# Loading the first 256 tokens of queries and keys as f32 through SyncE and ScalarE, with a new global order, in a fused attention and gated-MLP kernel

## The chip, the cores and the metric

The kernel runs on one core of a Trainium2 chip. That core has a matrix engine (TensorE, PE), a vector engine (VectorE, DVE), a scalar engine (ScalarE, ACT), a general engine (GpSimd, POOL) and a synchronisation engine (SyncE, SP). Each engine runs its own instruction stream in order, and streams wait for each other only through semaphores. Transfers between HBM and on-chip memory are issued from the POOL, SP or ACT stream; those from POOL can change the data type on the way. The metric is the device time of one execution in microseconds (us), lower is better.

## The reference

The inputs are q, k, v of shape 4 x 8 x 768 x 64 (batch, heads, tokens, head size) and four weight matrices, all f32. Attention is computed first; heads 0, 2 and 6 see all earlier tokens, the other five see the 4 first tokens and a window of 64. Its result, 3072 tokens by 512 features, goes through a gated MLP.

```
scores = matmul(q, k.T) / 8
keep   = causal                                   # heads 0, 2, 6
keep   = causal & (key < 4 | query - key < 64)    # the other heads
x      = softmax(where(keep, scores, -1e9)) @ v   # as (3072, 512)

g    = x @ w_gate                                 # 512 x 1536
val  = x @ w_val                                  # 512 x 1536
gate = sigmoid(x @ w_res)                         # 512 x 512
out  = x + gate * ((gelu(g) * val) @ w_out)       # 1536 x 512
```

## The kernel before

**Chunks.** The 3072 tokens are worked on in six chunks of 512 (`CHUNKS`, lines 25 to 32), four tiles of 128 tokens each. Chunk 0 is tokens 0 to 511 of batch 0. For each chunk the kernel transposes q and k so that the head size lies on partitions (qT, kT), computes scores, exponentials, masks, the weighted sum of v, the normalisation, the transposed result xT, and then the gated MLP with f16 operands. Heads are taken in four pairs, `PAIRS = ((0, 2), (4, 6), (1, 3), (5, 7))`; chunk 0 takes them in the order pair 0, 2, 1, 3. Chunk 0 also works in two halves of 256 tokens: for its first four blocks of hidden features (f0 to f3), the gate and value products of half 0 are tasks of their own that can run while the attention of half 1 is not finished.

**Tasks and the order.** The program is a graph of tasks. Each task is a few instructions on one engine, with a list of tasks that it depends on. The order is not found when the kernel is built: the string table `PLAN` lists task numbers in one global order (lines 51 to 119), `PLACES` names the slot of each buffer, `schedule` (line 255) walks the list and appends each task to its engine's stream, and `assign_waits` puts in the semaphore waits that the dependencies need. A letter behind a number picks the engine where a task may run on more than one (a ACT, d DVE, g POOL, s SP). An entry w39 puts in 39 fillers (line 1414): matmuls of 256 columns on a zeroed tile that nobody reads and that keep PE busy. So an engine takes its tasks in the order of `PLAN`, and a task at the head of a stream that is not ready holds back all behind it.

**Loads of chunk 0.** All loads of q, k, v and of the weights are issued by POOL (`dma`, line 537; they appear as L539), because they turn f32 into f16 on the way. `loads_rows` (line 641) loads q and k of chunks 0 and 1. In chunk 0 the first 256 tokens (y = 0) come as two transfers of four heads for k and two for q, the next 256 tokens (y = 1) as one transfer each. Eight PE tasks `qkT` (L682, eight transposes of 128 by 64 each) and eight copies `qkE` (L693, 128 x 512, PSUM to SBUF, on DVE or ACT) then make kT and qT. `values` (line 606) loads v by tiles; the copies `vs` (L617) and `vk` (L598) arrange parts of v for the window heads. Nine small POOL instructions build the identity and two mask tiles (L497 to L525); the causal mask needs two of them, the window mask six and a copy on DVE (L508, `spread`).

**Attention and MLP lines.** Scores are L850, sink scores L941, exponentials L866 and L870, masks L902 (`mask0` for pair 0 is the first; it needs the causal mask). Weighted sums are L974 and L477, reciprocals L1028, `norm16` L1039, `norm` L1041, transposes of the result L1063 with their copies L1071 (`xE`). In chunks 3 to 5 half of that transpose is one DMA transpose issued by SP (L1054, `xD`). PE's gate and value products are L477 and L478: the helper `mm` issues one matmul over the whole array, or two over halves of 64 columns, as the mode of the array stands. DMA transposes of q and k from chunk 2 on are L726 (`dT`), also on SP.

**What PLAN gives around the start.** The streams before begin like this (names as above; K and Q for k and q, a and b for the two transfers of a matrix; gN and vN are the gate and value products of feature block fN, h0 and h1 the two halves):

```
POOL  K(y1) Ka Qa Kb Q(y1) 3 consts Qb v0 v1 3 consts wv0 4 consts v3 3 vk v2 vk wg0
      Q(chunk 1) Q(chunk 1) wg1 wv1 wg2 wv2 wr K K wo ...
PE    w39 T(y1 K) w2 T(y0 K) w4 T(y0 Q) T(y1 K) w6 scores ... w and T and scores mixed ...
      attention of h0 ... v1 v3 g3 g1 (h0), rest of h1, g0, T(chunk 1), g2 ...
DVE   E(y1 K) E(y0 Q) E(y1 K) E(y0 K) E(y1 Q) E(y1 Q) mask0 spread vs mask1 mask1 vs ...
```

77 fillers are placed, 39 of them at the very start.

Of the kernel before, what the change touches and what calls it, by code (L numbers as in the profile page):

```python
# [4 lines left out]
NHEAD = 8  # L5
# [425 lines left out]
def build_kernel(nc, q, k, v, w_gate, w_val, w_out, w_res, out):  # L431
# [153 lines left out]
    def values(b, a, z, base, each, on_engines=False):  # L585
# [43 lines left out]
        for lo in cuts:  # L629
            hi = lo + 1 if each else z  # L630
            ts = []
            for dst, src, off in ((0, 64, 1), (64, 0, 0)):
# [4 lines left out]
                ts[-1].late = 2.5  # L637
            for i in range(lo, hi):
                BB.vstok[i] = ts

    def loads_rows(c, si, b, a, z):

        BB = batch(b)
# [867 lines left out]
```

## Time and profile before

| | us |
|---|---|
| median of 3 runs | 266.2 (265.41 to 267.15) |
| profiled execution, its span from first to last instruction | 264.3 |
| PE busy | 254.5 |
| DVE busy | 210.8 |
| ACT busy | 155.3 |
| POOL busy | 106.8 |

The profile gives the execution's own time as its span. The median of the runs is 1.9 us above it. PE is busy in 96% of the span, but busy time also holds the fillers, and the share is a mean over stages with different limits; the start, up to about 30 us, has its own.

### The profile page before, as it was taken

What the parts mean: (1) busy time and instruction counts of PE and PEld (TensorE: products, weight loads), DVE (VectorE), ACT (ScalarE), POOL (GpSimd) and SP (SyncE); (2) the same over time, 40 slices, a digit from 0 to 9 for tenths busy, and PEclk for the clock granted to TensorE, in tenths of its full rate; (3) what the DMA queues carried; (4) which work ended last, traced back from release to release, by engine and by line L of the source; (5) the groups of instructions that cost most, each with busy time, mean ns of one, the idle gap of its engine ahead of it and who ended that gap; (6) DMA issues with size and microseconds to landing.
All of it is one profiled execution on the core that took longest, in us unless ns stands there. A gap on an engine that the chain in (4) does not pass through costs nothing.

```text
span 264.3 us, 8077 instructions
## 1 busy us (share of the span) xinstructions
PE 254.5 (96%) x3421; PEld 180.7 (68%) x3421; DVE 210.8 (80%) x473; ACT 155.3 (59%) x274; POOL 106.8 (40%) x145
## 2 busy tenths in 40 slices
PE   8999999999999999999998899999999998999993
PEld 5657655558567578667677477579588677778891
DVE  1499555999988978678999677999687976877985
ACT  1277534964554998564883356884655995445511
POOL 8996741990000998013976620711500111110021
PEclk9999999999999999999999999999999999999998
DMA  7999999999297999968999994899589509050004
GB/s 69 166 139 178 207 196 191 188 158 115 82 271 99 141 123 135 182 154 182 136 97 124 152 138 93 200 123 104 69 92 237 101 2 122 7 77 2 2 2 159
DMA packets 102067, 33.17 MB, mean 125 GB/s; under 512 B 88720, under 2 KB 97168, under 8 KB 102032
## 3 DMA queue, kind: packets, MB, share of 16 engines
q0 software_dynamic: 74704, 18.88, 77.3%
q1 hardware_dynamic: 26896, 13.26, 25.0%
q8 instruction: 27, 0.44, 0.7%
q10 hardware_dynamic: 432, 0.52, 0.5%
q14 instruction: 8, 0.07, 0.1%
HBM read 29.36 MB, written 10.49 MB: 151 GB/s over the span
## 4 chain that ended last, share of the span: by engine, by line
PE 87%; DVE 8%; DMA 3%; issue 1%; ACT 0%; DVEq 0%
PE ps L477 45%; PE ps L478 30%; PE ps L850 4%; PE ps L1414 4%; DMA xT<-x 3%; PE ps L682 2%; PE ps L974 2%; PE ps L1063 1%; DVE xtok L1041 1%; DVE x L1039 1%; DVE vk L598 1%; PE ps L941 1%; DVE hS L1251 0%; DVE hT L1228 0%; DVE vs L617 0%
## 5 line engine op out<-in xcount | busy, mean ns | idle before, releaser
L539 POOL DMA_DIRECT2D qks<-in_q_dram x37 | 33.2, 983 | 48.3 <-DMA qT<-qks 26.1
L1359 POOL DMA_DIRECT2D out_dram<-otile x16 | 15.6, 975 | 76.8 <-DVE otile L1355 66.2
L477 PE MATMUL ps<-xT,wg 128*128 128x512 f16 (+1 forms) x172 | 38.7, 337 | 1.4 <-DMA xT<-x 1.0
L477 PE MATMUL ps<-xT,wv 128*128 128x512 f16 (+1 forms) x172 | 38.5, 337 | 0.0
L1129 ACT ACTIVATE gact<-ps 128x512 f16<-128x512 f32 x38 | 22.1, 596 | 27.0 <-PE ps L477 18.0
L1131 DVE SCALAR_TENSOR_TENSOR hT<-gact,ps 128x512 f16<-128x512 f16 x38 | 25.8, 683 | 13.7 <-ACT gact L1129 5.8
L539 POOL DMA_DIRECT2D qks<-in_k_dram x37 | 34.8, 977 | 1.4 <-POOLq L1493 0.8
L1203 DVE TENSOR_TENSOR ps<-ps,otile 128x256 f32<-128x256 f32 x60 | 24.0, 428 | 7.7 <-PE ps L477 3.7
L1221 ACT ACTIVATE gact<-ps 128x512 f16<-128x512 f32 x30 | 16.6, 596 | 15.7 <-PE ps L477 10.8
L539 POOL DMA_DIRECT2D va<-in_v_dram x24 | 23.7, 1017 | 3.8 <-DVE va L534 3.8
L477 PEld LDWEIGHTS ps<-xT,wg 128*128 128x128 f16 x172 | 16.2, 98 | 13.1 <-DMA xT<-x 1.5
L477 PEld LDWEIGHTS ps<-xT,wv 128*128 128x128 f16 x172 | 16.6, 98 | 11.4 <-issue 0.2
L866 ACT ACTIVATE ea<-ps 128x1024 f16<-128x1024 f32 (+2 forms) x24 | 22.0, 925 | 1.4 <-PE ps L850 1.3
L1228 DVE SCALAR_TENSOR_TENSOR hT<-gact,ps 128x512 f16<-128x512 f16 x30 | 19.3, 682 | 2.6 <-PE ps L478 1.2
L1299 ACT ACTIVATE srs<-ps 128x512 f32<-128x512 f32 x22 | 13.1, 599 | 12.2 <-PE ps L478 7.8
L477 PE MATMUL ps<-wo,hT 128*128 128x256 f16 (+1 forms) x114 | 18.3, 296 | 0.0
L478 PE MATMUL ps<-xT,wg 128*64 128x512 f16 (+1 forms) x144 | 17.6, 344 | 0.0
L478 PE MATMUL ps<-xT,wv 128*64 128x512 f16 (+1 forms) x144 | 17.6, 344 | 0.0
L1041 DVE TENSOR_TENSOR xtok<-ps,rcp 128x512 f32<-128x512 f32 (+1 forms) x28 | 16.8, 608 | 0.6
L1331 DVE TENSOR_TENSOR otile<-otile,ps 128x256 f32<-128x256 f32 x33 | 13.1, 412 | 3.7 <-PE ps L477 2.4
L850 PE MATMUL ps<-qT,kT 64*128 64x64 f16 (+4 forms) x391 | 15.9, 213 | 0.1
L478 PE MATMUL ps<-wo,hT 128*64 128x256 f16 x216 | 15.6, 273 | 0.4 <-DVE otile L1325 0.4
(175 smaller groups left out, 590.4 us busy)
## 6 DMA issues: line engine op xcount, KB each, us to landing
out_dram<-xtok SPq DMA_DIRECT2D x4, 1024.0 KB, 4.8
out_dram<-otile POOLq DMA_DIRECT2D x16, 256.0 KB, 4.5
va<-in_v_dram POOLq DMA_DIRECT2D x24, 128.0 KB, 5.6
qks<-in_k_dram POOLq DMA_DIRECT2D x32, 64.0 KB, 4.9
qks<-in_q_dram POOLq DMA_DIRECT2D x32, 64.0 KB, 5.0
wv<-in_moe_w_val_dram POOLq DMA_DIRECT2D x3, 512.0 KB, 13.2
wg<-in_moe_w_gate_dram POOLq DMA_DIRECT2D x3, 512.0 KB, 11.4
wo<-in_moe_w_out_dram POOLq DMA_DIRECT2D x4, 384.0 KB, 20.9
```

The source lines that it names most:

```text
L477: return e.matmul(o, lhsT=lhsT, rhs=rhs, **k)
L478: return [e.matmul(o[h:h + 64], lhsT=lhsT[:, h:h + 64], rhs=rhs, **k) for h in (0, 64)][-1]
L539: return G.add(eng, issue, lambda e: e.dma_start(out_ap(), in_ap), deps, prio, bufs=bufs, dma=cost, name=name, grp=grp)
L850: return [e.matmul(at(scr)[:, oo:oo + w], lhsT=side(BB, qb, low, 1)[half, k0:k0 + 128], rhs=side(BB, qb, low, 0)[half, qq:qq + w], start=T ...
L866: return e.activation(out=o, in_=i_, func=AF.Exp, scale=SM_SCALE)
L1041: t2 = G.add("dve", c_dve(2 * n * 64), lambda e: e.tensor_tensor(out=xview(), in0=avv(0, DHEAD), in1=scale(), op=ALU.mult), [t1] + xdeps, ...
L1129: ta = G.add("act", c_act(512), (lambda gb=gb, ga=ga, gw=gw: lambda e: e.activation(out=at(ga)[:, :], in_=at(gb)[:, gw], func=AF.Gelu))(), ...
L1131: th = G.add("dve", c_dve(512), (lambda vb=vb, ga=ga, f=f, vw=vw: lambda e: e.scalar_tensor_tensor(out=hv(f), in0=at(ga)[:, :], scalar=0.5 ...
L1203: return G.add("dve", c_dve(256), lambda e: e.tensor_tensor(out=at(ps)[:, o], in0=at(ps)[:, BL], in1=at(es)[:, 0:256], op=ALU.add), deps, ...
L1221: ta = G.add("act", c_act(512), (lambda x=x, ga=ga, both=both: lambda e: e.activation(out=two(at(ga)[:, :]), in_=both(x), func=AF.Gelu))() ...
L1228: th = G.add("dve", c_dve(512), (lambda x=x, f=f, ga=ga, both=both: lambda e: e.scalar_tensor_tensor(out=two(hv(f)), in0=two(at(ga)[:, :]) ...
L1359: t = G.add("pool", 1.0, (lambda ot=ot, r0=r0: lambda e: e.dma_start(out[r0:r0 + 128, :], at(ot)[:, :], accum_op=ALU.add))(), ends + [stor ...
```

## The change

The first 256 tokens of q and k of chunk 0 no longer come through POOL. A new function `loads_first` loads them as f32 into the staging tiles, one transfer of 128 KB for each head pair (two heads, 256 tokens): four for k issued by SP, four for q issued by ACT. A cast per transfer (`c16`, 128 x 256, f32 to f16, on any of DVE, ACT, POOL) writes f16 tiles borrowed from the pool of the tile x16; the same four PE tasks and four copies as before then make kT and qT. `loads_rows` keeps the second 256 tokens, as one transfer of k and one of q into one shared staging tile. The transposing transfers of the last chunk share a semaphore by token tile.

`PLAN` and `PLACES` are replaced as a whole: the order of every engine is another one, and tasks change engine where they may. 42 fillers are placed instead of 77, 14 of them at the start. At the start the streams become:

```
SP    four f32 loads of k (pairs 2, 0, 3, 1), then the copies of v of chunk 1
ACT   four f32 loads of q (pairs 2, 0, 3, 1), cast Q2, E(y0 K), cast K1, exp0, 2 sink exp,
      exp3, exp1, exp1, E(y1 Q), exp2, vs, ...
POOL  3 consts Q(y1) const v0 const K(y1) v1 const v3 K(chunk 1) 2 consts v2 const(causal)
      Q(chunk 1) Q(chunk 1) 3 vk wg0 wv0 vk wg1 wv1 wg2 v K wv2 wr v wo ...
DVE   cast K2, Q0, K0, E(y0 Q), cast K3, Q3, Q1, memset, E(y0 Q), E(y0 K), spread, mask0,
      mask3, mask1, mask1, E(y1 Q), E(y1 K), vs, ...
PE    w14 T(y0 Q) T(y0 K) w3 scores T(y0 Q) T(y0 K) w6 scores ... attention of h0 and h1,
      three T(chunk 1), g0, g2, g1, g3 (h0), last xT, then v3 v1 (h0), v2 g2 g0 ... (h1)
```

Six of the eight casts run on DVE, two on ACT. Of the four `vs` copies, two move from DVE to ACT. Neither order has fillers behind the last xT of chunk 0; there the order after still has four products of half 0 to do (v3, v1, v0, v2) and already has one T of chunk 1 more behind it than the order before. The core of the diff:

```diff
+    def loads_first(b, a):
...
+        st, half = [Buf(P_st), Buf(P_st)], [Buf(P_x16), Buf(P_x16)]
+        view = lambda j, p: at(st[j])[:, :].bitcast(FP32)[:, p * 256:(p + 1) * 256]
...
+        for p in ORDER:
+            h = PAIRS[p][0]
+            for j, src, eng in ((1, k, "sp"), (0, q, "act")):
+                ld = G.add(eng, 0.6, (lambda src=src, j=j, p=p, h=h: lambda e: e.dma_start(
+                    view(j, p).rearrange("p (x w) -> p x w", x=2),
+                    src[b, h:h + 3:2, lo:lo + 256, :].rearrange("x (p i) d -> p x (i d)", i=2)))(),
+                    [], -60, bufs=[st[j]], dma=0.5, name="ldf")
+
+                def cast(on, j=j, p=p):
+                    return lambda e: (e.activation(out=h16(j, p), in_=view(j, p), func=AF.Copy) if on == "act" else
+                                      e.tensor_copy(out=h16(j, p), in_=view(j, p)))
+                tok[j, p] = G.flex({e: (0.4, cast(e)) for e in ("dve", "act", "pool")}, [ld], -205, bufs=[st[j], half[j]], name="c16")
+        for k_ in (0, 2):
+            ps_ = sorted(ORDER[k_:k_ + 2])
+            for j in (1, 0):
...
+                tt = G.add("pe", 0.3, (lambda scr=scr, j=j, ps_=ps_: lambda e: [
+                    e.transpose(out=at16(scr)[64 * x:64 * x + 64, (m * 2 + i) * 128:(m * 2 + i + 1) * 128],
+                                in_=h16(j, p)[:, x * 128 + i * 64:x * 128 + i * 64 + 64], identity=ident[:, :])
+                    for m, p in enumerate(ps_) for i in range(2) for x in range(2)])(),
+                    [t_ident] + [tok[j, p] for p in ps_], 40 * k_ - 205, bufs=[half[j], scr], name="qkT")
...
     def loads_rows(c, si, b, a, z):
...
-        for y in range((z - a) // 2):
+        first = 0 if c else 1
+        assert (z - a) // 2 - first == 1
+        for y in range(first, (z - a) // 2):
...
                 t = G.add("sp", 1.65, (lambda sv=sv, to=to, o0=o0: lambda e: e.dma_start(
-                    at(to)[:, :, o0:o0 + 128], sv(), transpose=True))(), ds, base, bufs=[st, to], dma=0.85, name="dT")
+                    at(to)[:, :, o0:o0 + 128], sv(), transpose=True))(), ds, base, bufs=[st, to], dma=0.85, name="dT",
+                          grp=("dT", b, i) if c == len(CHUNKS) - 1 else None)
...
+            if c == 0:
+                loads_first(b, a)
             (loads_rows if c < ROWS_UNTIL else loads_natural)(c, si, b, a, z)
```

More of the change, by code (lines that the diff above doesn't have):

```diff
@@ L639, in values, with ev, fn @@
                 BB.vstok[i] = ts
+    def loads_first(b, a):
+        BB = batch(b)
+        lo = a * 128
+        qb, qo = qplace[b, a]
+        tok = {}
+        st, half = [Buf(P_st), Buf(P_st)], [Buf(P_x16), Buf(P_x16)]
+        view = lambda j, p: at(st[j])[:, :].bitcast(FP32)[:, p * 256:(p + 1) * 256]
+        h16 = lambda j, p: at(half[j]).rearrange("p c i k -> p (c i k)")[:, p * 256:(p + 1) * 256]
+        for p in ORDER:
[12 more added lines that the diff above has]
+            for j in (1, 0):
+                scr = Buf(P_ps, "scr0")
+                to, o0 = (BB.kt, lo) if j else (qb, qo)
+                tt = G.add("pe", 0.3, (lambda scr=scr, j=j, ps_=ps_: lambda e: [
[3 more added lines that the diff above has]
+                    [t_ident] + [tok[j, p] for p in ps_], 40 * k_ - 205, bufs=[half[j], scr], name="qkT")
+                tt.mode = "col"
+                def ev(on, scr=scr, to=to, o0=o0, ps_=ps_):
+                    def fn(e):
+                        o = at(to)[:, ps_[0]:ps_[1] + 1:ps_[1] - ps_[0], o0:o0 + 256].rearrange("c m (p i) -> c m p i", i=2)
+                        i_ = at16(scr)[:, 0:512].rearrange("c (m i p) -> c m p i", m=2, i=2)
+                        return e.tensor_copy(out=o, in_=i_) if on == "dve" else e.activation(out=o, in_=i_, func=AF.Copy)
+                    return fn
+                t = G.flex({"dve": (c_dve(512), ev("dve")), "act": (c_act(512), ev("act"))}, [tt], 40 * k_ - 205,
+                           bufs=[scr, to], name="qkE")
+                for p in ps_:
+                    for i in range(a, a + 2):
+                        (BB.ktok if j else BB.qtok)[p, i] = t
@@ L641, in loads_rows @@
     def loads_rows(c, si, b, a, z):
         BB = batch(b)
-        st = [Buf(P_st), Buf(P_st)] if c == 0 else [Buf(P_st)] * 2
+        st = Buf(P_st)
         base = {0: -60, 1: -15, 2: 50}[c]
@@ L647, in loads_rows, with sv, piece @@
         tok = {}
-        def sv(j, h0, h1, y):
-            if c == 0:
-                return at(st[j])[:, :].rearrange("p (h w) -> p h w", h=NHEAD)[:, h0:h1, y * 128:y * 128 + 128]
-            return at(st[j])[:, :].rearrange("p (j h w) -> p j h w", j=2, h=NHEAD)[:, j, h0:h1, :]
-        def piece(j, h, i, y):
-            o = h * 256 + y * 128 if c == 0 else (j * NHEAD + h) * 128
-            return at(st[j])[:, o + i * 64:o + (i + 1) * 64]
-        for y in range((z - a) // 2):
-            lo = (a + 2 * y) * 128
-            for gi, (h0, h1) in enumerate(((0, 4), (4, 8)) if c == 0 and y == 0 else ((0, 8),)):
-                for j, src in ((1, k), (0, q)):
-                    t = dma("pool", base + 4 * gi + 8 * y + 1 - j, (h1 - h0) * n * (0.092 if c else 0.089),
-                            (lambda j=j, h0=h0, h1=h1, y=y: lambda: sv(j, h0, h1, y))(),
-                            src[b, h0:h1, lo:lo + 256, :].rearrange("h (p j) d -> p h (j d)", j=n), bufs=[st[j]])
-                    t.late = 1.0 if c else 0.7
-                    for h in range(h0, h1):
-                        tok[j, h, y] = t
+        def sv(j):
+            return at(st)[:, :].rearrange("p (j h w) -> p j h w", j=2, h=NHEAD)[:, j]
+        def piece(j, h, i):
+            o = (j * NHEAD + h) * 128
+            return at(st)[:, o + i * 64:o + (i + 1) * 64]
+        first = 0 if c else 1
+        assert (z - a) // 2 - first == 1
+        for y in range(first, (z - a) // 2):
+            lo = (a + 2 * y) * 128
+            for j, src in ((1, k), (0, q)):
+                t = dma("pool", base + 8 * y + 1 - j, NHEAD * n * 0.092, (lambda j=j: lambda: sv(j))(),
+                        src[b, :, lo:lo + 256, :].rearrange("h (p j) d -> p h (j d)", j=n), bufs=[st])
+                t.late = 1.0
+                for h in range(NHEAD):
+                    tok[j, h, y] = t
         values(b, a, z, base + (10 if c == 0 else 2), False, c == 0)
         per = 2 if c == 0 else 4
-        for y in range((z - a) // 2):
+        for y in range(first, (z - a) // 2):
             lo = (a + 2 * y) * 128
@@ L679, in loads_rows, with tr @@
                     to = BB.kt if js[0] else qb
-                    def tr(e, items=items, scr=scr, y=y):
+                    def tr(e, items=items, scr=scr):
                         return [e.transpose(out=at16(scr)[64 * x:64 * x + 64, (m * n + i) * 128:(m * n + i + 1) * 128],
-                                            in_=piece(jj, h, i, y), identity=ident[:, :])
+                                            in_=piece(jj, h, i), identity=ident[:, :])
                                 for m, (p, jj) in enumerate(items) for i in range(n) for x, h in enumerate(PAIRS[p])]
                     tt = G.add("pe", c_mm(128, n) * len(items), tr, [t_ident] + [tok[jj, h, y] for p, jj in items for h in PAIRS[p]],
-                               pr, bufs=[st[js[0]], scr], name="qkT")
+                               pr, bufs=[st, scr], name="qkT")
                     tt.mode = "col"
```

153 rows, old and new, of tables (PLACES, PLAN) are left out of this document.

## The prediction, made before the changed kernel had run

> **What bounds the kernel now.** First I read the stretches of busy time (start and length of the stretch, then PE, weight loads, DVE, ACT, POOL, each with its instructions, clock, DMA share, GB/s):
>
> ```profile
> 8.16:13.67 5.51, 5.51 (x97) 3.75 (x97) 3.36 (x5) 2.23 (x4) 5.11 (x14) 1.00 1.77 169
> 13.67:23.50 9.83, 9.30 (x151) 5.92 (x149) 9.39 (x29) 7.67 (x17) 9.79 (x14) 1.00 1.43 145
> 23.50:29.33 5.83, 5.66 (x102) 4.62 (x103) 5.10 (x20) 3.95 (x7) 1.99 (x4) 1.00 1.33 206
> 29.33:140.00 110.67, 110.67 (x1164) 72.38 (x1163) 91.16 (x199) 71.82 (x123) 55.94 (x72) 1.00 1.36 155
> 140.00:180.00 40.00, 37.52 (x489) 26.92 (x489) 33.32 (x74) 24.22 (x44) 14.83 (x19) 1.00 1.19 136
> 180.00:259.10 79.10, 78.03 (x1379) 61.42 (x1373) 65.66 (x145) 43.56 (x80) 10.98 (x14) 1.00 0.44 71
> ```
>
> From 29.33 to 259.10 PE is the bound: 226.2 of 229.8 us busy, 3.6 idle. That body does the same work after the change, so the time can fall in two places: the start up to 29.33, and those 3.6 us. Then the chain of waits, in order of time:
>
> ```profile
> 1.21 7.03 PE ps L1414 x39
> 8.23 0.34 PE ps L682 x8
> ...
> 14.28 0.41 DVE ea L902
> ...
> 22.14 0.85 DVE vs L617
> ...
> 23.67 1.03 PE ps L477 x8
> ...
> 44.12 1.01 PE ps L682 x32
> ```
>
> The start has two parts. Up to 13.7 us the chain is PE, in its order of fillers and transposes: 39 fillers hold the first transposes until 8.23. From 13.7 to 23.5 it is DVE, 9.39 of 9.83 us busy, though PE shows 95% there. That the fillers and not the loads set 8.23 follows from POOL's issues and the landing of the first two:
>
> ```profile
> 1.35 1.89 POOL L539 DMA_DIRECT2D qks<-in_k_dram  x2 [0.83 <-POOLq L1493]
> 9.43 0.82 POOL L539 DMA_DIRECT2D wv<-in_moe_w_val_dram  x1
> 13.41 0.87 POOL L539 DMA_DIRECT2D va<-in_v_dram  x1
> 14.79 0.75 POOL L539 DMA_DIRECT2D wg<-in_moe_w_gate_dram  x1
> ...
> DMA to landing us min/median/max: 4.1/4.3/4.5
> DMA to landing us min/median/max: 7.5/7.5/7.5
> ```
>
> The first landing line is that of the two k transfers: the first k landed at 1.35 + 4.5 = 5.85, well before 8.23. The second is that of wg0 alone.
>
> **The first transposes.** Four transfers each leave SP and ACT; POOL loses four issues of 0.8 to 1.1 us. Neither queue issued a load before, so the nearest rows bound it (size, us to landing):
>
> ```profile
> out_dram<-otile ACTq DMA_DIRECT2D x2, 128.0 KB, 1.8
> out_dram<-otile SPq DMA_DIRECT2D x2, 128.0 KB, 2.0
> vs<-va SPq DMA_DIRECT2D x4, 113.8 KB, 4.7
> 73.85 0.61 SPq L633 DMA_DIRECT2D vs<-va  x1
> L693 ACT ACT_TABLE_LOAD x1 | 1.3, 1283 | 0.8 <-PEq L1493 0.8
> ```
>
> So 1.8 us on idle queues and 4.7 on loaded ones. At the start little else is in flight; I take 2.0 and keep 4.7. SP issues from 0.9 on, 0.6 apart, so K2 and K0 land at 2.9 and 3.5. ACT first has its table load (0.8 to 2.1), if that stands ahead of the issues: Q2 and Q0 land at 4.1 and 4.7, all eight by 6. A cast of 128 x 256 has no row. The nearest on DVE, with the other instructions ahead of the first mask, are these:
>
> ```profile
> L508 DVE COPY m_win<-m_win 128x128 f16<-128x128 f16 x1 | 0.2, 191 | 0.0
> L1039 DVE TENSOR_TENSOR x<-ps,rcp 128x256 f16<-128x256 f32 x8 | 3.3, 420 | 0.1
> L693 DVE COPY qT<-ps 128x512 f16<-128x512 f16 x3 | 2.1, 692 | 1.4 <-PE ps L682 1.3
> L508 DVE COPY m_win<-m_win 128x256 f16<-128x256 f16 x1 | 0.5, 522 | 0.0
> 1.32 0.49 DVE L532 MEMSET vk<- 128x520 f16 x1 [0.17 <-DVE blank L511]
> ```
>
> Between 0.19 and 0.42; I take 0.35, nearer to the f32 row, on ACT too. The first transposes then start near 4.7 + 0.4 = 5.1, where 14 fillers are long through, against 8.23. With 4.7 to land they start near 7.8.
>
> The row speaks against a rule here. The Trainium skill, "DMA: Bandwidth & Descriptors", section "Specifications", gives about 1 us to the first byte for GpSimd's path and 0.6 for SyncE's and ScalarE's; an estimate from it makes the new path 0.4 us quicker, where the rows have 4.5 against 1.8 to 2.0. No run yet shows a load on the new path.
>
> **DVE behind it, the term that counts.** DVE's first mask (mask0) ends the free part: all behind it was DVE-bound before. Ahead of mask0 DVE now has six casts (2.1), three copies E (2.1), a memset (0.49) and the window copy (0.52): 5.2 us from 4.6 on, so ready at 9.8. But mask0 also needs the causal constant, and that now comes on POOL behind seven loads. POOL has 7 x 0.87 = 6.1 us of loads and nine constant instructions; L497's six take:
>
> ```profile
> 5.60:11.62 6.02, 2.04 (x6) 1.00 1.91 165
> ```
>
> With three memsets, each below the 0.49 above, that is about 2.8, so the constant is ready at 1.35 + 6.1 + 2.8 = 10.3. Hence the casts cost nothing: POOL's 10.3 covers them with 0.5 us to spare; without that cover they would cost up to 2.1. Mask0 starts at 10.3, against 14.28 in the chain: 4.0 us earlier.
>
> From mask0 to the end of the last norm16 of half 1 DVE took 12.7 us before:
>
> ```profile
> 14.28:27.00 12.72, 12.23 (x42) 1.00 1.42 157
> L1028 DVE RECIPROCAL rcp<-ps 128x4 f32<-128x4 f32 x8 | 1.3, 172 | 0.1
> L1071 DVE COPY xT<-ps 128x256 f16<-128x256 f16 x5 | 1.3, 286 | 0.7 <-PE ps L1063 0.7
> L1101 DVE SCALAR_TENSOR_TENSOR hT<-gact,ps 128x256 f16<-128x256 f16 x3 | 1.2, 402 | 0.0
> L617 DVE COPY vs<-va 64x455 f16<-64x455 f16 x2 | 0.8, 422 | 0.0
> ```
>
> The same stretch after the change gains work: three copies E (3 x 0.69), three norms (3 x 0.42), two reciprocals (2 x 0.17), two xE (2 x 0.29) and a small window copy (0.19): 4.4. It loses the first window copy (0.52), two vs copies moved to ACT (0.42, and 0.85 by the chain) and two products of h (2 x 0.40): 2.6. Neighbours overlap by some 0.08 us each, which takes the net of 1.8 to 1.6. So it ends at 10.3 + 12.7 + 1.6 = 24.6, and PE's last xT at about 25.0. Four products of half 0 are left then that were done before (in the chain two of them, eight matmuls at 23.67, take 1.03, so 2.0), and one T of chunk 1 is already done (two take 1.01 at 44.12, so 0.5). The state of 29.33 is reached at 25.0 + 2.0 - 0.5 = 26.5: **2.8 us earlier**, if nothing in between waits.
>
> That PE allows it, and where it may not, follows from its fillers, which ran at two rates (in all 39 in 7.03 us, then 38):
>
> ```profile
> 5.00:6.00 1.00, 1.00 (x7) 0.73 (x5) 1.00 1.84 178
> 7.00:8.00 1.00, 1.00 (x12) 0.86 (x9) 1.00 1.76 170
> ```
>
> Seven touch the early microsecond and twelve the later one, about 0.2 and 0.11 us each, while the clock column says 1.00 in both. Of PE's 21.2 us from 8.16 to 29.33, 38 fillers of 0.11 are 4.2 and 0.7 is idle, so 16.3 is work; 16.3 - 1.5 + 28 x 0.11 = 17.9 from 5.1 on ends at 23.0, 2.0 before 25.0. That reserve is needed. Before, PE was busy without a gap from 1.21 on. After, it runs 14 slow fillers (3.0 us) to 4.2 and then stands until 5.1, so the slow stretch should last longer. At half rate the first four T (0.34 each) and their scores and fillers, about 2.7 us, take 5.4, and the second exponential and mask3 come 1.5 us late, on DVE's path. I charge 0.5, between 0 and 1.5, as the same stretch of DVE before holds such waits already (12.72 less 12.23): **2.3 us** is left.
>
> The Trainium skill, "TensorE: Matmul & The Clock Gate", Part 1, has this as a clock gate that opens after about 3.4 us of sustained activity in a free-running window; by it a gap at 4.2 would put full rate off to 9 us or so, the upper end of that charge. The trace agrees as far as the two rates go.
>
> **The other moves.** The chunk-1 loads of q and k need the two f32 tiles, free once the casts are done (about 8); POOL comes to the first at 8, so this costs 0 to 0.5 and is covered by transposes that need them only near 20. The vs copies on ACT add 1.3 us there; it was busy 7.67 of 9.83 us in DVE's stretch, so it stays below DVE. The gate matrix wg0 is issued at about 13.5, behind the constant (10.3), two loads (1.7) and three small copies and their waits (some 1.5), instead of 14.79. The shared semaphores of the last chunk make a reader of kT wait for qT too, which its scores need anyhow: 0. The end of the order is the same but for one addition moved to POOL: 0.
>
> **The body.** Its idle time of 3.6 us falls to these waits of PE:
>
> ```profile
> PE ps L478 <- issue: 1.1, 1, 1.1
> PE ps L477 <- DMA xT<-x: 1.0, 1, 1.0
> PE ps L1063 <- DVE x L1039: 0.7, 1, 0.7
> ```
>
> The new order may close or open such gaps. In PLAN, the DMA transposes of q and k stand further ahead of their scores than before, so transfers have more cover; the three xT transposes have about as much as before. I take 0.3 saved, between 3.6 saved and 3 lost.
>
> **Sum.** 2.3 + 0.3 = 2.6; 264.3 - 2.6 = 261.7 for the span. The median lay 1.9 above the profiled span: **263.6 us**.
>
> **Rivals.**
>
> *The start gives nothing.* Loads land after 4.7 us, PE stays slow, and the casts lose their cover: 2.7 us later loads leave about 1.3 of the 2.8, and mask3's 1.5 takes that. Time 266, as before. For it: the 4.7 row and the half rate. Against it: POOL's constant at 10.3 hides late loads up to 0.5 us anyhow, and the queues are nearly empty at the start. Chance 0.22.
>
> *Start and body both gain.* The start gives 2.8 and the body's waits mostly go: 264.3 - 2.8 - 2.3 + 1.9 = 261.1. For it: more cover for the transfers. Against: the waits named issue and L1039 are no transfers. Chance 0.18.
>
> *Slower: the value matrix comes late.* Before, wv0 was issued at 9.43, ahead of wg0; now it follows wg0, at about 14.5. The median landing of wv is this:
>
> ```profile
> wv<-in_moe_w_val_dram POOLq DMA_DIRECT2D x3, 512.0 KB, 13.2
> ```
>
> PE needs wv0 at v3, at 25.0, with the last xT done and every later task behind it. With the 7.5 us of wg0 it lands at 22.0, in time; with 13.2 it lands at 27.7 and costs 2.7, so 266.3; it makes the kernel slower than before by 1% from a landing at 30.3 on, that is if the f32 loads and v, all ahead of it, push it back to 15.8 us. Against it: the 13.2 belongs to transfers with three other matrices in front. Chance 0.13.
>
> *The forecast*, 262.4 to 265 around 263.6, has 0.47.
>
> **How the numbers follow.** The range reaches down to the second rival's lower half (2.8 and all 3.6 give 259.8; I stop at 260.5) and up to 267.5, past the first rival and the milder case of the third; some 2 in 10 is outside. About 1% is what a measurement of this kernel can tell from no change: 263.5 and 268.9. Faster by over 1%: the second rival and just over half of the forecast, 0.43. Slower: the worse cases of the third, 0.10. The rest, 0.47, is within 1%.
>
> **What would show it.** Right: first transposes near 5, the first mask near 10.3, released by POOL's constant, DVE over 95% busy from there to 24.6, and PE dense from about 25. Wrong: first transposes after 7; DVE waiting for exponentials around 11 to 13; PE waiting for a weight matrix at 25; or PE idle in the body well off 3.6 us.

## The result, and the profile after

The changed kernel takes 263.1 us in the median (262.4 to 263.6), the kernel before measured beside it 265.5 (264.5 to 267.2): a ratio of 0.990, with a 95% interval of 0.988 to 0.994. The prediction was 263.6 us. Where an execution of a kernel fell into a slower state, as one of e2 and two of e3f below did, its time is left out. The time and its sign were right; the place where the time fell was not. The prediction had 2.3 us from the start and 0.3 from the body. The traces have it the other way round.

To split the gain between the two I use one number for the start: how much PE work is still to do at 29.33 us, the moment at which the order before had its dense body. The stretches of busy time (as in the prediction: start and end of the stretch, its length, then PE, weight loads, DVE, ACT, POOL, clock, DMA share, GB/s) give it. First the kernel before, from 29.33 us to the end:

```profile
29.33:264.30 234.97, 227.06 (x3036) 161.30 (x3034) 192.09 (x418) 140.20 (x247) 82.91 (x104) 1.00 1.00 123
```

Then the changed kernel; 256.46 is where its last product starts, as 259.30 was before:

```profile
0.00:29.33 29.33, 24.68 (x366) 16.98 (x367) 20.45 (x64) 18.50 (x33) 26.34 (x45) 1.00 1.37 180
29.33:140.00 110.67, 110.67 (x1174) 72.12 (x1173) 90.11 (x200) 72.10 (x123) 56.82 (x73) 1.00 1.55 162
140.00:180.00 40.00, 40.00 (x584) 28.93 (x584) 32.71 (x75) 24.72 (x45) 10.66 (x13) 1.00 0.91 117
180.00:256.46 76.46, 75.70 (x1275) 61.06 (x1271) 60.29 (x134) 43.23 (x81) 9.54 (x12) 1.00 0.40 66
29.33:261.90 232.57, 227.22 (x3040) 162.69 (x3038) 185.71 (x409) 140.56 (x249) 77.99 (x98) 1.00 1.03 122
```

PE has 227.22 us of work left at 29.33 us where it had 227.06. So the start is no further along: the gain there is -0.2 us. This is one execution. Experiment e6 below has the same instructions up to 120 us, and in its execution 226.34 us are left: a gain of 0.7. Either way it is far from 2.3, and the last section shows that PE's clock differed between the two. What fell is PE's idle time behind it: 234.97 less 227.06 is 7.91 us before, 232.57 less 227.22 is 5.35 after, 2.56 us less (2.7 in e6's execution). (Both sums hold the tail of some 5 us, in which PE has nearly nothing to do.) Of the waits of the body that the prediction quoted, the answer for PE after 28 us keeps two small ones:

```profile
PE ps L477 <- issue: 0.4, 1, 0.4
PE ps L892 <- DVE hT L1270: 0.3, 1, 0.3
```

Why the start gave so little is in the chain of waits of the changed kernel's first 30 us (start, length, what; L658 are casts, L666 the first transposes, L1456 the fillers, L1081 the norm16 of before's L1039):

```profile
2.39 6.09 DMA qks<-in_q_dram
8.50 0.30 DVE x L658
8.85 1.07 PE ps L666 x16
9.92 1.40 PE ps L1456 x6
...
13.10 0.77 ACT eb L912 x2
13.90 0.59 DVE eb L944 x2
...
26.53 0.43 DVE x L1081
...
27.87 2.21 PE ps L476 x20
```

The last f32 load was issued at 2.39 us and took 6.09 to land, so it was in at 8.48, where the prediction had all eight in by 6. Behind it stand the second group of transposes and six fillers, both at PE's slow rate (1.07 us for 16 transposes). PE is dense from 27.87 and not from 25 (in e6's execution from 25.43). The landing times of the eight loads (L651), then one POOL load and the first mask in order of time:

```profile
DMA to landing us min/median/max: 2.8/4.1/6.1
...
9.26 0.88 POOL L538 DMA_DIRECT2D qks<-in_k_dram  x1 [2.08 <-DVE x L658]
11.93 0.43 DVE L944 TENSOR_TENSOR ea<-ea,m_causal 128x512 f16<-128x512 f16 x1 [0.91 <-POOL m_causal L496]
```

POOL stood still for 2.08 us with the first key load of chunk 1, whose tile the late casts had not yet left, and the causal constant was queued behind it. So the first mask, which the constant releases, began at 11.93 and not at 10.3.

### The profile page after: what moved, and what is told of

Read it like the earlier page. It is cut to its first block, busy times and chain, and to the rows that moved or that the text cites. A ratio compares the mean times of both kernels' runs of the same rounds, so it can differ in the third digit from the quotient of the medians.

```text
span 261.9 us, 8050 instructions
## 1 busy us (share of the span) xinstructions
PE 251.9 (96%) x3404; PEld 179.7 (69%) x3404; DVE 206.2 (79%) x472; ACT 159.1 (61%) x282; POOL 104.3 (40%) x142
## 4 chain that ended last, share of the span: by engine, by line
PE 88%; DVE 7%; DMA 2%; issue 1%; ACTq 1%; ACT 0%; DVEq 0%
PE ps L476 47%; PE ps L477 31%; PE ps L892 5%; DMA qks<-in_q_dram 2%; PE ps L1105 1%; PE ps L1016 1%; DVE x L1081 1%; PE ps L983 1%; DVE xtok L1083 1%; PE ps L1456 1%; ACTq L651 1%; DVE otile L1397 1%; DVE hT L1270 0%; DVE kT L734 0%; PE ps L666 0%
## 5 line engine op out<-in xcount | busy, mean ns | idle before, releaser
L1401 POOL DMA_DIRECT2D out_dram<-otile x16 | 14.5, 904 | 95.7 <-DVE otile L1397 63.5
L476 PE MATMUL ps<-xT,wv 128*128 128x512 f16 (+1 forms) x168 | 37.5, 339 | 0.0
L538 POOL DMA_DIRECT2D qks<-in_k_dram x35 | 28.8, 842 | 15.1 <-PE ps L723 8.2
L538 POOL DMA_DIRECT2D qks<-in_q_dram x35 | 30.2, 902 | 7.8 <-DMA qT<-qks 7.8
L538 POOL DMA_DIRECT2D va<-in_v_dram x24 | 24.3, 1021 | 12.4 <-PE ps L476 12.4
L1341 ACT ACTIVATE srs<-ps 128x512 f32<-128x512 f32 x22 | 12.9, 599 | 12.3 <-PE ps L477 8.6
L1241 ACT ACTIVATE ps<-ps 128x256 f32<-128x256 f32 x25 | 9.3, 371 | 16.2 <-PE ps L476 11.8
L1373 DVE TENSOR_TENSOR otile<-otile,ps 128x256 f32<-128x256 f32 x33 | 13.7, 418 | 6.5 <-PE ps L477 4.3
L477 PE MATMUL ps<-xT,wv 128*64 128x512 f16 (+1 forms) x152 | 18.5, 340 | 0.0
L892 PE MATMUL ps<-qT,kT 64*128 64x64 f16 (+4 forms) x391 | 17.1, 216 | 0.8 <-DVE kT L734 0.5
## 6 DMA issues: line engine op xcount, KB each, us to landing
wv<-in_moe_w_val_dram POOLq DMA_DIRECT2D x3, 512.0 KB, 12.4
```

Of the source, the lines that this page charges most:

```text
L476: return e.matmul(o, lhsT=lhsT, rhs=rhs, **k)
L477: return [e.matmul(o[h:h + 64], lhsT=lhsT[:, h:h + 64], rhs=rhs, **k) for h in (0, 64)][-1]
L538: return G.add(eng, issue, lambda e: e.dma_start(out_ap(), in_ap), deps, prio, bufs=bufs, dma=cost, name=name, grp=grp)
L892: return [e.matmul(at(scr)[:, oo:oo + w], lhsT=side(BB, qb, low, 1)[half, k0:k0 + 128], rhs=side(BB, qb, low, 0)[half, qq:qq + w], start=T ...
L1401: t = G.add("pool", 1.0, (lambda ot=ot, r0=r0: lambda e: e.dma_start(out[r0:r0 + 128, :], at(ot)[:, :], accum_op=ALU.add))(), ends + [stor ...
```

## The experiments

My theory was that the order of the body made the gain, and that the start lost its 2.3 us to late f32 loads, to POOL's order and to PE's slow clock. The rival was that the start made the gain after all. Every experiment was timed against the kernel before, which took 265.7 to 266.0 us in those groups of runs. "Left" and "idle" come from one profiled execution of each kernel. "Left" is PE work left at 29.33 us, "idle" is span less 29.33 less left. (The line numbers of the experiments lie a few off those of the changed kernel: L651 there is L656 here, L658 is L663, L666 is L671, L1456 is L1461. In e1, e1b and e7 they lie three or four off those of the kernel before.)

| kernel | median us | ratio to before, 95% interval | left | idle |
|---|---|---|---|---|
| before | 265.5 | | 227.06 | 7.91 |
| changed | 263.1 | 0.990 (0.988 to 0.994) | 227.22 | 5.35 |
| e1 old start, new order behind it | 283.3 | 1.066 (1.060 to 1.071) | 230.55 | 19.72 |
| e1b the same, later seam | 266.0 | 1.001 (0.998 to 1.004) | 226.89 | 8.18 |
| e2 new start, old order behind it | 270.7 | 1.019 (1.013 to 1.025) | 227.59 | 12.18 |
| e2b the same, later seam | 270.1 | 1.019 (1.014 to 1.024) | 228.85 | 11.42 |
| e3 constants before the K load | 263.7 | 0.993 (0.990 to 0.996) | 227.14 | 5.63 |
| e3b constants before all POOL loads | 261.4 | 0.984 (0.980 to 0.988) | 224.90 | 5.17 |
| e3f e3 with nine more fillers | 263.2 | 0.992 (0.988 to 0.995) | 228.19 | 5.88 |
| e6 loads beside the xT transfer | 263.5 | 0.992 (0.988 to 0.995) | 226.34 | 5.23 |
| e7 before, loads earlier | 265.7 | 1.000 (0.997 to 1.003) | 226.73 | 8.14 |
| e9 e3b, two loads back in front | 264.3 | 0.995 (0.992 to 0.997) | 228.73 | 5.04 |
| e10 e3b, key copy on ACT | 262.1 | 0.986 (0.982 to 0.990) | 225.37 | 5.60 |
| e11 e10 without late fillers | 262.6 | 0.988 (0.984 to 0.992) | 225.76 | 4.91 |

**Half of each order (e1, e2, and e1b, e2b).** `PLAN` is cut and joined: the tasks of one order up to a point, then all others in the other order. In e1 and e2 the cut is behind the last xE of chunk 0, in e1b in the attention of chunk 1, in e2b at the first products of chunk 1. Buffers taken after the cut get the slots of the other kernel where they are free.

```diff
 e1, e1b: loads, functions and PLAN of before up to the cut
-         rest of PLAN of before
+         PLAN of the changed kernel, less what is done (fillers left out)
 e2, e2b: loads_first and PLAN of the changed kernel up to the cut
-         rest of its PLAN
+         PLAN of before, less what is done (fillers left out)
```

> The kernel before up to the last transpose and copy of its first chunk's normalized tokens (fp16 loads by GpSimd, old order), and from there the order of the changed kernel. Theory (the 2.3 to 2.8 us were saved in the body, where PE's idle time fell from 3.6 to 0.7 us, and the start gave nothing): about 263.0, ratio to before 0.990, PE idle after 29.33 us at most 1.2 us. Rival (the start gave the gain): about 265.5, ratio 1.000.

> The changed kernel up to the last transpose and copy of its first chunk's normalized tokens (f32 loads, casts on chip), and from there the order of the kernel before. Theory (body): about 265.5, ratio 1.000, PE idle in the body again 3 to 4 us. Rival (start): about 263.0, ratio 0.990.

Both missed both numbers, and the waits say why. PE's longest wait in e1, and its place in e1's chain:

```profile
PE ps L685 <- DMA qks<-in_k_dram: 10.3, 1, 10.3
...
21.61 18.69 DMA qks<-in_k_dram
```

The old start issues the keys of chunk 1 behind the weights, at 21 us; the new order wants them before. In e2, PE waited for transfers again:

```profile
PE ps L482 <- DMA xT<-x: 1.3, 1, 1.3
PE ps L988 <- DMA qT<-qks: 1.1, 1, 1.1
PE ps L897 <- DMA q<-qT: 0.9, 1, 0.9
```

The seam, not the theory, was measured in e1. So the seam was moved to where no load runs short:

> As the first experiment, but the seam lies later, at a place where the kernel before has every load done that the changed kernel's order needs soon: the order of the kernel before (fp16 loads, old start and first products), then the changed kernel's order, in which PE's idle time fell. Theory (the body gave the gain): 262.7 to 263.5, ratio 0.990, PE idle after 60 us at most 1.2 us. Rival (the start gave it): 265.3 to 266.0, ratio 1.000. A third outcome, over 267, would say that an order fits only behind its own start.

> The changed kernel's start and first products, then the order of the kernel before, with the seam at a place that leaves no load short. Theory (body): 265.3 to 266.0, with PE idle 3 to 4 us in the body again, first of all 1 us for the transposed tokens near 149 us. Rival (start): 262.7 to 263.5. Third outcome, over 267: an order fits only behind its own start.

e1b came out at the rival's time (266.0), e2b at the third outcome (270.1). By time alone e1b speaks for the rival. PE's waits of e1b after 60 us say more:

```profile
PE ps L481 <- issue: 1.4, 1, 1.4
PE ps L1066 <- DVE rcp L1031: 1.0, 1, 1.0
PE ps L977 <- DVE xtok L1044: 0.9, 1, 0.9
PE ps L853 <- DVE hT L1231: 0.3, 1, 0.3
```

The two waits for DVE fall at the seam, at 62 to 64 us. Behind it the new order leaves 0.3 us of waits for other engines where the order before had 2.5 (the 3.6 us idle in its body, less the 1.1 named issue), but a wait named issue is there again, of 1.4 us; the last section comes back to it. So the new order takes 2.2 us of such waits out of the body, and 1.9 us are given back at the seam. e1b and e2b do not prove the theory; they show that, cut at these places, neither half of the order has a gain of its own.

**The transfers beside xT (e6, e7).** Before, the first DMA transpose of xT (at 142.46 us) took 7.4 us to land, with six POOL loads just ahead of it; after (141.56) it took 3.3, with none. e6 puts seven loads back beside it, e7 moves a store behind the six loads in the kernel before (1195 is the transfer of xT in e6; 1129, 1126, 1117 and 1114 are stores; the others that move are loads).

```diff
 e6: PLAN of the changed kernel
-... 1177 410 409 366 1189 369 1180 ... 1125 412 364 ... 1188 370 391 1207 ... 1195 1133 1129 1126 ...
+... 1177 1189 1180 ... 1125 364 ... 1188 1207 ... 1195 1133 1129 410 409 366 369 412 370 391 1126 ...
 e7: PLAN of before
-... 1155 1117 1118 ... 340 ... 349 ... 350 ... 368 ... 372 ... 401 ... 1192 1114 ...
+... 1155 1118 ... 340 ... 349 ... 350 ... 368 ... 372 ... 401 ... 1192 1117 1114 ...
```

> The changed kernel with seven of GpSimd's loads (keys, queries and values of a later chunk), which it issues at 130 to 135 us, issued at 137.7 to 143 instead, about where the kernel before has six: beside SyncE's transposing transfer of the normalized tokens at 141.56. Theory (transfers out of the way of that one gave part of the body's gain): its landing rises from 3.3 to 6 to 8 us as in the kernel before (7.4), PE waits 2 to 3.5 us for it at 145, time 265 to 266.5. Rival (the order of the products alone made the gain): landing or not, PE wait under 0.5 us, time 263.1.

> The kernel before with one move on GpSimd: the store of 136.80 us, which waits 1.56 us for the gated output, stands behind six loads of keys and queries instead of ahead of them, so that these are issued from 135.2 on and not up to 142.2. Theory: the transposing transfer of 142.46 lands in 4 to 5.5 us instead of 7.4, PE's wait of 1.05 us at 148.8 goes, time 264.4 (1.0 under the kernel before). Rival (that transfer is slow by itself): landing over 6.5 us, time unchanged at 265.5.

Both went against the theory. The landing of that transfer in e6, then in e7 the same and PE's wait near it:

```profile
DMA to landing us min/median/max: 4.3/4.3/4.3
```

```profile
DMA to landing us min/median/max: 7.1/7.1/7.1
...
PE ps L481 <- ACT otile L1330: 1.5, 1, 1.5
```

With the loads beside it the transfer landed 1.0 us later, PE did not wait, and the time is that of the changed kernel within the spread. The landing did not reach the 6 to 8 us of the theory, so e6 does not say what a slow landing would cost. In e7 it stayed slow, PE's wait for it went, and one of 1.5 us took its place: the store that was moved back held its tile, ACT waited for the tile and PE for ACT. So the loads' place near xT is not what made the gain. Which of the many moves in the order did is open.

**The start (e3, e3b, e9).** These change POOL's order alone. e3 moves the masks' constants ahead of the key load that waited (256), and this load one place back; e3b does the same and moves all constants ahead of all POOL loads; e9 is e3b with two loads back at the front.

```diff
 e3
-... 221 239 ... 421 256 230 ... 434 9 10 238 11 ... 426 4 432 257 ...
+... 221 9 10 4 239 ... 421 230 ... 434 238 256 11 ... 426 432 257 ...
 e3b
-... 218 16 215 217a 6 235 15 2 213 w14 228 236 7 234 237 ... 229 8 ...
+... 218 6 2 7 8 9 10 4 235 16 215 217a 15 213 w14 228 236 234 237 ... 229 ...
 e9
+... 218 235 236 6 2 7 8 9 10 4 16 215 217a 15 213 w14 228 234 237 ... 229 ...
```

(2, 4 and 6 to 10 are constants, 234 to 239 and 256 POOL loads.)

> The changed kernel with one move on GpSimd: the three instructions that make the window's and the causal mask's constants stand ahead of the first load of the second chunk's keys, which waits 2.08 us for a cast. Theory (that wait held the first mask back: 11.93 where 10.3 was predicted): the causal constant by 7.5 us, the first mask at 10.9 to 11.1 released by DVE's own copies or PE, last norm16 about 0.8 us earlier (25.7), time 262.3 (0.8 less than the changed kernel's 263.1). Rival (exponentials and the slow clock bound the start, not the constant): first mask earlier but the later masks wait for ACT, last norm16 within 0.2 us of 26.53, time 263.1.

> The changed kernel with all of GpSimd's constants ahead of all of its loads, so its loads are issued about 2 us later. Theory (the f32 loads of the second pair of heads landed late, 4.9 to 6.1 us after issue, since GpSimd's loads ran beside them): they land in 4 to 5 us, the second group of transposes starts at 7.5 to 8.0 instead of 8.85, first mask about 10.2, time 261.8 to 262.3. Rival (the f32 loads are slow by themselves): second group still at 8.7 to 8.9, and the later GpSimd loads make the transposes of the second half of the chunk wait beyond 13.0, time 263 to 264.

In e3 the first two masks, in order of time:

```profile
11.10 0.42 DVE L949 TENSOR_TENSOR ea<-ea,m_causal 128x512 f16<-128x512 f16 x1
...
13.21 0.43 DVE L949 TENSOR_TENSOR es<-es,m_win 128x512 f16<-128x512 f16 x1 [1.70 <-ACT es L913]
```

The first mask came 0.8 us earlier, as expected, and the second waited 1.70 us for its exponential: the rival's outcome, work left 227.14. PE got its full rate at about the same time as in the changed kernel, near 12.3 and 12.8 us. In e3b, the landing of the f32 loads, the second group of transposes, the first mask, and the stretch from 29.33 us:

```profile
DMA to landing us min/median/max: 2.7/3.8/4.7
...
7.50 0.64 PE L671 MATMUL ps<-ident,x 128*64 128x128 f16 x16 [0.44 <-DVE x L663]
9.29 0.42 DVE L949 TENSOR_TENSOR ea<-ea,m_causal 128x512 f16<-128x512 f16 x1
...
29.33:259.40 230.07, 224.90 (x3019) 160.61 (x3017) 185.01 (x406) 139.71 (x246) 76.17 (x96) 1.00 1.06 123
```

The last f32 load lands 1.4 us sooner, the second group starts 1.35 us sooner and runs at the full rate, the first mask is at 9.29, and 2.3 us less work is left. Not all of that need be POOL's order: PE had its full rate from 5.7 us on in this execution and from 12.8 on in that of the changed kernel. In e11 below, which has POOL's order of e3b but for one load, two other moves that brought no gain, and the full rate only from 12.4 on, 1.5 us less work is left than in the changed kernel. The time is 1.8 us below the changed kernel: the fastest version here, 1.6% below the kernel before. Two causes were joined in it, the constants' place and that of the loads, so e9 takes them apart:

> The kernel of the fourth experiment (all constants ahead of all of GpSimd's loads; 261.4) with two of those loads put back to the front, so that they are issued at 1.7 to 4 us, beside the f32 loads, and all constants right behind them (done by about 5.8 us, long before the first mask at 9.3). Theory (the f32 loads were late because GpSimd's loads ran beside them): the last f32 query lands in 5.5 to 6.1 us after its issue instead of 4.7, the second group of transposes starts at 8.3 to 8.9 instead of 7.5, work left at 29.33 us 226 to 227 instead of 224.9, time 262.3 to 263.2. Rival (the constants' place made the gain): second group within 0.2 us of 7.5, time 261.4.

The same rows of e9, and one stretch of busy time:

```profile
DMA to landing us min/median/max: 2.7/4.5/6.8
...
9.55 1.06 PE L671 MATMUL ps<-ident,x 128*64 128x128 f16 x16 [2.46 <-DVE x L663]
...
29.33:263.10 233.77, 228.73 (x3054) 163.81 (x3051) 187.14 (x413) 141.67 (x251) 76.79 (x97) 1.00 1.03 122
...
9.14:15.96 6.82, 6.41 (x77) 3.90 (x79) 4.06 (x10) 3.90 (x10) 5.98 (x11) 0.50 2.08 168
```

With two POOL loads beside the f32 loads, the last of these takes 6.8 us, PE waits 2.46 us for its cast, and the time is 264.3. Theory and sign hold; the loss was larger than expected. PE's clock may add to it: the last row puts it at half from 9.14 to 15.96 us in this execution (in that of e3b it is 1.00 there); how much it adds is not shown. The medians, over twelve and six executions, are 2.9 us apart. The Trainium skill, "DMA: Bandwidth & Descriptors", section "Issuing engines are not separate DMA queues", says that transfers from SyncE, ScalarE and GpSimd run on the same 16 engines and interleave. The trace agrees: 4.7 us without POOL's first loads, 6.8 with two of them.

**PE's clock, and what else is on the chain (e3f, e10, e11).**

```diff
 e3f (on e3)
-... 213 w14 228 ... 221 9 10 4 239 232 ...
+... 213 w18 228 ... 221 9 10 4 239 w5 232 ...
 e10 (on e3b)
-... 236 234 237 ... 230 231 w6 ...
+... 236 237 234 ... 230 231a w6 ...
 e11 (on e10): the entries w3, w4 and w6 behind 14 us left out
```

> The third experiment's kernel (masks' constants ahead of the chunk's next key load; 263.7, no gain) with nine more fillers on PE in the two stretches in which it stood still for the casts: 18 instead of 14 ahead of the first transposes, and 5 ahead of the second group. Theory (PE lost its full rate by those gaps, and with slow transposes and six fillers of 1.4 us on the chain the earlier mask was worth nothing): the second group takes 0.64 us instead of 1.06, the six fillers behind it 0.8 instead of 1.46, scores and exponentials 0.8 to 1.1 us earlier, PE work left at 29.33 us about 226.2 instead of 227.1, time 262.7. Rival (only the late f32 loads count): work left within 0.2 us of 227.1, time 263.5.

> The kernel of the fourth experiment (261.4) with two more moves: the second group's key copy on ScalarE instead of DVE (where it stood behind the query copy), and the chunk's second load of values one place earlier on GpSimd. Theory (the start is a chain, and what is cut from it goes through to the end one for one): scores at 8.8 instead of 9.3, PE's wait of 0.7 us for values at 13.15 under 0.1, work left at 29.33 us 224.2 to 224.5 instead of 224.9, time 260.7 to 261.0. Rival (the next wait takes it up): work left 224.9, time 261.4.

> The kernel of the third line of this call (key copy on ScalarE, values earlier) without the 13 fillers that stand behind 14 us in PE's order, which lie on the chain of waits there (1.9 us in all). Theory: PE is at full rate by then and has work enough, so 0.3 to 0.8 us more is saved, time 260.0 to 260.6. Rival (they filled waits for DVE and kept PE's rate): no gain or a loss up to 1 us, 261 to 262.

e3f did what it should up to 10 us and lost it behind. PE in order of time, and the stretch of busy time at half clock:

```profile
5.43 0.64 PE L671 MATMUL ps<-ident,x 128*64 128x128 f16 x16 [0.65 <-DVE x L663]
...
9.66 0.83 PE L1461 MATMUL ps<-blank 128*128 128x256 f16 x6
...
11.45 0.82 PE L1461 MATMUL ps<-blank 128*128 128x256 f16 x3
...
27.09 0.27 PE L481 MATMUL ps<-xT,wg 128*128 128x256 f16 x1 [1.53 <-issue]
...
11.10:14.52 3.42, 3.42 (x51) 2.00 (x45) 1.62 (x5) 2.64 (x7) 3.25 (x8) 0.50 2.16 166
```

The transposes ran at 0.64 us from the first on, and six fillers took 0.83; then the rate fell to half (three fillers in 0.82), and at 25.6 PE stood still for 1.53 us in which no engine held it up. Without that gap, work left would be 228.19 less 1.53, 226.7, half of the way from e3's 227.1 to the expected 226.2. This execution took 265.1 us, where the median of its kernel is 263.2; by the medians e3f is 0.5 us below e3, where 1.0 was expected, and that is within their spread. The nine fillers moved the stretch at half rate, which ended near 12.3 us in e3 and at 14.5 here, and did not remove it. So e3f does not price the clock.

e10 and e11 went to their rivals (e11, at 262.6, a little beyond its own): no gain over e3b, though e3b's chain of waits named what they take away, the values' load and late fillers:

```profile
6.39 6.71 DMA va<-in_v_dram
...
18.38 0.76 PE ps L1461 x6
```

A row of that chain is no price. In e10 PE's wait of 0.71 us for the values is gone, and the scores that start at 14.84 in e3b start at 14.84 here too, now behind a copy on DVE. PE's full rate also came later in these two executions (last section), so they do not test the moves alone.

**Start and time together.** Over the eight kernels with the changed order, idle behind 29.33 us stays between 4.9 and 5.9 us, and the median moves with the work left, from 261.4 at 224.9 to 264.3 at 228.7 (0.8 us for each us; e3f and e6, whose profiled executions were far from their medians, lie up to 1 us off). The two with the old order at that place, before and e7, have the same work left as the changed kernel within 0.5 us and lie 2.4 to 2.6 us above its time; their idle time is 7.9 and 8.1. That is the body's share, and this comparison, not e1 and e2, carries it. It compares traces: the runs that changed the order behind the start alone (e1b, e6, e7) neither made the gain nor took it away, so which moves made it stays open.

## Why the prediction was right in time and wrong in its steps

- **"I take 2.0 and keep 4.7"** for the f32 landing is the step that failed. The eight took 2.8 to 6.1 us, the last of them beyond the upper bound. "At the start little else is in flight" was false: POOL's own first loads run beside them, and e3b and e9 show what these cost. The bounds came from rows of two to four transfers at other places, and not from eight at once beside POOL's.
- **The first transposes** at 5.44 (5.1 predicted) were nearly right, since the first four loads landed in about 3 us and ACT's table load ran behind its issues, not ahead. The prediction then let the second group follow at once; it started at 8.85, and the chain runs through it.
- **"This costs 0 to 0.5 and is covered"** for POOL's chunk-1 load: 2.08 us. The wait was seen and priced by the early casts; the late ones made it four times as long, and the causal constant behind it went from 10.3 to 11.8. By e3 this alone was worth nothing, as the exponentials were late too.
- **The slow clock** was charged 0.5, between 0 and 1.5. PE stayed slow until 12.8 us, well behind the 9 that the prediction allowed for at the upper end. Its price was not measured: in e6's execution, with full rate from 4.83 on but for 8.24 to 11.66, 0.9 us less work is left, but the last f32 load also landed 0.4 us sooner there. **"2.0 before 25.0"** of PE's reserve did not hold: PE is on the chain from 8.85 to 13.1.
- **From the first mask to the last norm16** 14.3 us were expected and 15.0 came, with 1.1 us of waits for exponentials on ACT in them. (The sum has a slip: by its own 0.08 us for each of the six instructions more, the net of 1.8 becomes 1.3 and not 1.6.)
- Together: **2.3 us** from the start became -0.2 (0.7 in e6's execution). The first rival had this part right. Its own sum is off, though: f32 loads 2.7 us later, less the 0.5 of cover, would leave 0.6 of the 2.8 and not 1.3.
- **The body's 0.3 saved** was mis-sized: 2.56, inside its bounds of 3.6 saved and 3 lost. That PE's waits would go was the second rival. The reason given, more cover for the transfers of q and k, is not what the runs bear out: of the waits that went, one was for xT, for which e6 and e7 show that the loads near it do not decide, and the largest was no transfer of data at all. Two of the prediction's own signs of being wrong came: DVE waited for exponentials up to 12.99 and up to 13.90 us, and PE's idle time from 29.33 to its last product was 0.8 us where it had been 3.6.
- **The weight matrices** came in time; no wait for them is in the trace, and the third rival fell.
- The offset of 1.9 us from span to median was 1.2 in the later runs of both kernels. Span against span, 261.7 was predicted and 261.9 came.

So two errors of about 2 us cancelled: that the time came out right is luck. With e3b the start gives 2.2 us over the kernel before (227.06 less 224.90), near the 2.3 that the prediction had promised.

## What to carry to other kernels

Ask of every early transfer what else is on the DMA engines, on all issuing queues: moving loads to a faster queue gains little while the old queue sends other loads beside them, and putting the old queue's arithmetic ahead of its loads gave more here (1.8 us) than the start of the change did (-0.2 to 0.7). Measure a start by the work of the bounding engine that is left at a fixed time, not by its first milestones: the first mask was 2.4 us earlier and the start no further. Read it in more than one execution: two with the same start differ by 0.9 us. An order found for a whole program is fitted end to end, so half of one joined to half of another tells of the seam first.

## What the runs showed of the hardware

**A wait of PE that no engine causes, behind an instruction transfer.** The waits of PE named issue, of 0.2 to 1.5 us, follow a transfer of 16 KB on the queue of kind instruction (q8). There are 18 of them behind the first 2 us in the fourteen traces, and each ends 2.2 to 3.1 us behind the start of such a transfer, 1.3 to 1.5 us behind its end. Most such transfers (some 27 in each trace) have no wait behind them. Before, the queue in the quarter microsecond from 221.00, and PE:

```profile
q8 instruction: 1, 0.02, 33.5%
...
223.98 0.44 PE L478 MATMUL ps<-vk,ek 128*64 128x65 f16 x16 [1.06 <-issue]
```

In e3f such a transfer lies in the quarter from 24.50 and PE resumes at 27.09; the changed kernel has the transfer at the same 24.50 and no gap there. Nine fillers ahead moved the place in the stream, and a gap of 1.53 us came up. So what PE runs short of there may be instructions. That is inferred from the order of events; no kernel was made to vary this alone. By it some 0.7 us of the body's gain (1.06 against 0.4) is a matter of where the stream happens to be cut.

**PE's rate after the same instructions is not the same.** e10 and e11 have one and the same PE stream up to 14 us. The first two runs of fillers after the second transposes in e10:

```profile
8.58 0.94 PE L1461 MATMUL ps<-blank 128*128 128x256 f16 x6
9.90 0.50 PE L1461 MATMUL ps<-blank 128*128 128x256 f16 x3
```

And in e11:

```profile
8.72 1.46 PE L1461 MATMUL ps<-blank 128*128 128x256 f16 x6
10.77 0.82 PE L1461 MATMUL ps<-blank 128*128 128x256 f16 x3
```

The full rate comes some 3 us apart (in e11 three fillers take 0.50 from 12.96 on). The changed kernel and e6 show it better, since there the times agree as well: both start their first transposes at 5.44 or 5.43 us, behind the same 14 fillers and a gap of 1.1 us. First the changed kernel, then e6 with two stretches of busy time:

```profile
5.44 1.06 PE L666 MATMUL ps<-ident,x 128*64 128x128 f16 x16 [1.14 <-DVE x L658]
```

```profile
5.43 0.64 PE L671 MATMUL ps<-ident,x 128*64 128x128 f16 x16 [1.13 <-DVE x L663]
...
4.83:8.24 3.41, 1.41 (x25) 0.91 (x25) 2.23 (x6) 0.94 (x3) 2.42 (x4) 1.00 1.53 206
8.24:11.66 3.42, 3.15 (x39) 2.03 (x40) 2.27 (x6) 0.77 (x2) 2.71 (x6) 0.50 2.16 166
```

So the rate is not a matter of the instructions and gaps alone. The clock column holds what the trace recorded of the granted clock, and reads 1.00 for the time ahead of an execution's first record, whatever the rate is. These records begin with the full clock, at 12.84 us in the changed kernel and at 4.83 in e6 (three fillers took 0.82 at 11.90 in the changed kernel and 0.50 at 13.79). Where the clock fell back at the start, in e3f, e6 and e9, it had been full for 6.82, 3.41 and 3.42 us, and it stayed at half for 3.42, 3.42 and 6.82: once or twice the same time. The Trainium skill, "TensorE: Matmul & The Clock Gate", Part 1, describes a window of about 3.4 us that runs freely and does not start with the kernel. The traces agree with both: the steps have that length, and they lie differently in the changed kernel and e6. No gap as long as the window was needed for the fall: in e6 PE was busy for 1.41 of the 3.41 us ahead of it, and the longest gap that touches these 3.41 us is one of 1.32.
